# Pooling the PSUM banks, spreading the up projections, and moving an addition to VectorE in a planned attention and MLP kernel

## The chip, the cores and the metric

One core of a Trainium2 chip. The metric is device time in microseconds (us), the median of the runs that are named. The record lists every run of this study as fast; all are compared as fast runs, each with runs of the kernel before on the same chip. TensorE (PE) does the matrix products and leaves them in eight PSUM banks (3 x 2 and 2 x 1 in the kernel before); VectorE (DVE) and ScalarE (ACT) empty the banks (an "evacuation"); GpSimd (POOL) works beside them.

## The reference, cut to what matters

```python
def reference(A_x, ...):                       # x is 1 x 2048 x 512
    def _A_ref(x, wq, wk, wv, wo, beta):       # 32 heads of 16, N = 4 segments of L = 512
        phi = lambda t: jnp.where(t > 0, t + 1.0, jnp.exp(t))
        ...
        for s in range(N):
            logits = jnp.einsum('bhqd,bhkd->bhqk', qs, ks) * scale + mask
            p = _softmax(logits, axis=-1)
            a_dot = jnp.einsum('bhqk,bhkd->bhqd', p, vs)
            pq = phi(qs)
            num = jnp.einsum('bhld,bhde->bhle', pq, M)
            den = jnp.einsum('bhld,bhd->bhl', pq, z)[..., None] + 1e-06
            o = g * (num / den) + (1.0 - g) * a_dot
            pk = phi(ks)
            M = M + jnp.einsum('bhld,bhle->bhde', pk, vs)
            z = z + jnp.einsum('bhld->bhd', pk)
        ...
        return o @ wo
    def _B_ref(x, w_gate, w_up, w_down):       # width 1792 = 14 pieces of 128
        return (_gelu(x @ w_gate) * (x @ w_up)) @ w_down
    x = A_x
    g = _sigmoid((x * gate_w).sum(-1, keepdims=True))
    return g * a + (1 - g) * b
```

Names in what follows: a logit group is q times k for one slot, a pv group is p times v (`a_dot`), an M group adds to M and z, `num` and `zbd` (z as a block-diagonal tile) belong to num and den, a mask is the causal zeroing of p on GpSimd, and a down group is the product with `w_down`.

Per segment there are 14 "up" pieces, each four matmuls of 128x512 on TensorE. So there are 56 up groups in all. phi is needed 12 times, each on a tile of 128x1024.

## The kernel before

The kernel is a list of tasks. A small planner in Python gives each task an engine and a place in that engine's order, from assumed durations; the order is fixed when the program is built. A task can start in the plan only when a buffer of its "ring" is free. PSUM is split into two rings:

```python
plg = ctx.enter_context(tc.tile_pool(name="plg", bufs=3, space=bass.MemoryType.PSUM))    # 3 x 2 banks
pgen = ctx.enter_context(tc.tile_pool(name="pgen", bufs=2, space=bass.MemoryType.PSUM))  # 2 x 1 bank
RINGS = {"lg": 3, "gen": 2, "qT": 3, "kT": 3, "kO": 3, "pT": 12, "E": 1, ...}
```

A logit slot takes two "lg" buffers (a pair of banks for each of two exponentials); nearly everything else shares the two "gen" banks. Slots are kept at least PACE apart:

```python
PACE = 1900
...
    # logit_slot(s, t)
    g = add("PE", 240, fn, prio=0, deps=deps, mode="row", alloc=["lg", "lg"], frees=frees,
            gap=(LT[gi - 1], PACE) if gi > 0 else None)
```

In the dense stage ahead of the first slot stand the q, k, v and gate products of segment 0 and the gate products of all segments (between the last GELU and the first exponential the trace has an ACT_TABLE_LOAD of 1.28 us on ScalarE, so the kernel keeps the two apart). Fourteen up groups stand there too (13 of them run before the first logit group):

```python
for s in range(NSEG):
    ...
    for hp in range(HS // 2):
        gate_pair(s, hp, 41 + 20 * s + hp)
        ...
        if s >= 2:
            up_group(*ups.pop(0), 41.5 + 20 * s + hp)
```

The other 42 are "fillers" between slots: all 28 of segments 1 and 2 in the first segment's slots, then 7, 7 and 0. The addition of phi is on GpSimd:

```python
def f_a(_):
    d = mk()
    nc.gpsimd.tensor_add(d[:, :, :], box["E"][:, :, :], box["Q"][:, :, :])
...
return add("POOL", 2250, f_a, prio=5, deps=[m, q], alloc=[ring], frees=[("E", e), ("Q1", q)])
```

The softmax here doesn't subtract the row's maximum and nothing guards it: scores larger than these inputs give would overflow.

## Time and profile before

| | kernel before |
|---|---|
| time, median of 15 runs | 290.55 us (289.91 to 291.34) |
| span of the profiled run | 289.2 us |
| TensorE, ScalarE, VectorE, GpSimd busy | 94%, 72%, 62%, 45% |
| first and last logit group start | 78.32 and 263.49 us |
| sum of the 79 slot intervals by TensorE's work | 172.3 us |
| excess of the trace over that sum | 12.9 us |

The last three rows are the ledger that the prediction sets up: each interval between logit groups is priced from what TensorE has to do in it, and what the trace has over that is the excess, which is stall but for some 0.8 us of rounding.

A timeline line reads: start in us, duration, engine, line of the kernel, operation, output<-inputs, shapes, xcount, and in brackets how long the engine sat idle before it and what ended that. A line of the list of waits reads: us in total, times, longest.

### The profile page before, as it was taken

The numbers are of one execution on the slowest core, as the hardware profiler recorded it, in microseconds if no ns is written. First come the engines' busy times: TensorE is split into PE (matmuls) and PEld (weight loads), VectorE is DVE, ScalarE is ACT, GpSimd is POOL, SyncE is SP. The second block draws the span as 40 slices with busy tenths as digits, with TensorE's granted clock in tenths as the row PEclk, the third lists the DMA queues.
The fourth block names the chain that finished last, engine by engine and source line by source line (L and its number), as shares of the span: only waits on it lengthen the run. The fifth ranks groups of instructions, "written<-read, shape, count | busy, mean of one in ns | idle before, by whom it ended". The sixth has DMA issues, their size and how long they took to land.

```text
span 289.2 us, 5673 instructions
## 1 busy us (share of the span) xinstructions
PE 272.4 (94%) x2279; PEld 118.1 (41%) x2320; DVE 178.8 (62%) x320; ACT 208.6 (72%) x227; POOL 130.0 (45%) x220
## 2 busy tenths in 40 slices
PE   7999999999998997999989999998899999999994
PEld 4444444444443443343334444333344344344441
DVE  2331212232197899888997786789986973869400
ACT  3634554424497998699998998999899999896021
POOL 8000000015037786755497657554855855556000
PEclk9999999999999999999999999999999999999999
DMA  7974960000001110100001330000000000000011
GB/s 241 325 125 79 363 211 2 0 0 2 0 2 36 36 24 18 39 0 2 0 2 31 27 51 25 14 8 2 0 20 20 0 20 18 22 22 18 20 36 37
DMA packets 22019, 13.74 MB, mean 48 GB/s; under 512 B 14056, under 2 KB 20968, under 8 KB 21992
## 3 DMA queue, kind: packets, MB, share of 16 engines
q1 hardware_dynamic: 21448, 12.85, 17.2%
q10 hardware_dynamic: 544, 0.52, 0.5%
q8 instruction: 18, 0.29, 0.5%
q14 instruction: 9, 0.07, 0.1%
HBM read 8.13 MB, written 2.10 MB: 35 GB/s over the span
## 4 chain that ended last, share of the span: by engine, by line
PE 67%; DVE 17%; SPq 7%; DMA 2%; POOL 2%; issue 2%; ACT 1%; ACTq 0%
PE dn L828 16%; PE up L324 14%; PE gt L324 12%; SPq L233 7%; PE lg L575 7%; PE pv L626 6%; PE dn L833 5%; PE k L324 2%; DVE T L644 2%; PE q L324 2%; DVE vz L176 2%; DVE G L495 2%; DVE Nm L817 2%; POOL pT L607 1%; DVE Tm L813 1%
## 5 line engine op out<-in xcount | busy, mean ns | idle before, releaser
L598 ACT ACTIVATE pT<-lg 128x1024 bf16<-128x1024 f32 x160 | 154.2, 1027 | 15.2 <-PE lg L575 14.0
L607 POOL TENSOR_SCALAR_AFFINE_SELECT pT<-pT 128x512 bf16<-128x512 bf16 (+1 forms) x160 | 93.2, 593 | 72.2 <-ACT pT L598 71.2
L495 DVE TENSOR_TENSOR G<-up,G 128x512 bf16<-128x512 f32 x56 | 38.0, 683 | 41.1 <-PE up L324 41.1
L324 PE MATMUL up<-xT,wup 128*128 128x512 bf16 x213 | 55.2, 380 | 3.1 <-DVE G L495 1.9
L485 ACT ACTIVATE G<-gt 128x1024 bf16<-128x1024 f32 x28 | 28.7, 1023 | 36.1 <-PE gt L324 36.1
L828 PE MATMUL dn<-wdn,G 128*128 128x512 bf16 x213 | 52.2, 380 | 1.9 <-DVE vz L176 0.7
L324 PE MATMUL gt<-xT,wga 128*128 128x512 bf16 x217 | 50.9, 379 | 0.4
L324 PEld LDWEIGHTS <-wga 128*128 128x128 bf16 x224 | 21.8, 98 | 26.2
L324 PEld LDWEIGHTS <-wup 128*128 128x128 bf16 x224 | 19.9, 97 | 27.9 <-issue 8.2
L828 PEld LDWEIGHTS <-G 128*128 128x128 bf16 x224 | 20.2, 98 | 26.9 <-issue 5.9
L456 POOL COPY G<-tt 32x16 f32<-32x16 f32 x16 | 3.1, 195 | 56.9 <-DVE tt L448 56.3
L644 DVE STREAM_TRANSPOSE T<-pv 128x512 f32<-128x512 f32 x32 | 22.7, 711 | 9.0 <-PE pv L626 8.9
L626 PE MATMUL pv<-pT,vz 128*32 128x256 bf16 (+2 forms) x640 | 23.4, 275 | 0.4
L575 PE MATMUL lg<-qT,kT 16*128 16x256 bf16 (+2 forms) x320 | 18.7, 273 | 0.1
L575 PE MATMUL lg<-qT,kO 32*128 32x128 bf16 (+2 forms) x320 | 18.0, 272 | 0.1
L421 PE MATMUL v<-wv,xT 128*128 128x512 bf16 x61 | 15.5, 379 | 2.7 <-DVE vz L176 1.6
L833 PE MATMUL dn<-wo,xT 128*128 128x512 bf16 x63 | 16.2, 379 | 0.2 <-issue 0.2
L626 PEld LDWEIGHTS <-vz 128*32 128x32 bf16 x640 | 12.6, 96 | 8.8 <-issue 1.3
L869 ACT ACTIVATE osb<-dn,omz 128x512 bf16<-128x512 f32 x6 | 4.1, 686 | 16.6 <-PE dn L833 16.6
L324 PE MATMUL q<-xT,wq 128*128 128x512 bf16 x59 | 15.4, 380 | 0.2
L575 PEld LDWEIGHTS <-kT 16*128 16x128 bf16 x320 | 7.3, 92 | 20.0 <-issue 19.3
L699 POOL TENSOR_TENSOR pq<-E,Q 128x1024 bf16<-128x1024 bf16 x6 | 12.8, 2140 | 4.0 <-DVE E L695 4.0
(88 smaller groups left out, 249.9 us busy)
## 6 DMA issues: line engine op xcount, KB each, us to landing
out_dram<-osb SPq DMA_DIRECT2D x16, 128.0 KB, 1.7
wup<-in_B_w_up_dram SPq DMA_DIRECT2D x1, 1792.0 KB, 8.0
wdn<-in_B_w_down_dram SPq DMA_DIRECT2D x1, 1792.0 KB, 13.4
wga<-in_B_w_gate_dram SPq DMA_DIRECT2D x1, 1280.0 KB, 11.1
wq<-in_A_wq_dram SPq DMA_DIRECT2D x1, 512.0 KB, 6.4
wga<-in_B_w_gate_dram SPq DMA_DIRECT2D x1, 512.0 KB
wv<-in_A_wv_dram SPq DMA_DIRECT2D x1, 512.0 KB, 8.3
wo<-in_A_wo_dram SPq DMA_DIRECT2D x1, 512.0 KB, 9.0
```

The lines of the kernel that those rows point to most:

```text
L233: nc.sync.dma_start_transpose(xT[:, fc, s * L:(s + 1) * L], x2[s * L:(s + 1) * L, fc * P:(fc + 1) * P])
L324: nc.tensor.matmul(t, lhsT=W[:, fc, c0:c0 + P], rhs=xT[:, fc, s * L:(s + 1) * L], start=(fc == 0), stop=(fc == FC - 1))
L421: nc.tensor.matmul(t[:, :], lhsT=xT[:, fc, s * L + kt * P:s * L + (kt + 1) * P], rhs=wv[:, fc, :], start=(fc == 0), stop=(fc == FC - 1))
L485: ge = evac("ACT", g, box, lambda e, t: nc.scalar.activation(dst, t[:, :, :], AF.Gelu_apprx_tanh), cost=960, ring="lg")
L495: UPT[(s, hs)] = evac("DVE", g, box, lambda e, t: nc.vector.tensor_mul(G[:, s, hs, :], t[:, :], G[:, s, hs, :]))
L575: nc.tensor.matmul(A[j // 2][:, j % 2, at * P:(at + nq) * P], lhsT=l, rhs=r, start=True, stop=True, tile_position=(32 * j, 0))
L598: nc.scalar.activation(pT[(s, t, h)][:, :, :], A[h][:, :, :], AF.Exp, scale=0.25)
L607: nc.gpsimd.affine_select(out=v, in_=v, pattern=pat, compare_op=ALU.is_ge, fill=0.0, base=0, channel_multiplier=-1)
L626: nc.tensor.matmul(t[32 * j:32 * j + 32, qb * P:(qb + nq) * P], lhsT=vz[s % 2][:, kt, h * VW:h * VW + 32], rhs=pT[(s, t0 + w, j // 2)][:, ...
L644: nc.vector.transpose(TT[key][:, e, :, :].rearrange("p a b -> p (a b)"), t[:, :])
L828: nc.tensor.matmul(t[:, :], lhsT=G[:, s, hs, qt * P:(qt + 1) * P], rhs=wdn[:, hs, :], start=(hs == 0), stop=stop and (hs == HS - 1))
L833: nc.tensor.matmul(t, lhsT=xT[:, c, s * L + qt * P:s * L + (qt + 1) * P], rhs=wo[:, c, :], start=first and c == 0, stop=(c == NCH - 1))
```

## The change

The intent is to let TensorE stall less in the slots. There are 672 lines of diff; the core of it has four parts.

One: all eight PSUM banks in one tile, any single bank for a dense group and any two adjacent ones for half a logit slot. The planner guards the slot's two pairs:

```diff
+SHAPES = {"gen": [(b,) for b in range(NBANK)],
+          "pair": [(b, b + 1) for b in range(NBANK - 1)]}
...
+    ps = pps.tile([P, NBANK, L], F32, name="ps", tag="ps")
...
+        def take(kind, used, at, hold, mode):
+            best = None
+            guard = kind == "gen" and mode != "row" and nleft and due is not None
+            if guard:
+                g = [1e12 if b in used else guess(b) for b in range(NBANK)]
+                lim = due + SLACK
...
+            for q in SHAPES[kind]:
...
```

Two: all 56 up groups between the slots, and a pace that divides the dense work that is left by the slots that are left:

```diff
+NUPS = (28, 10, 9, 9)
-            if s >= 2:
-                up_group(*ups.pop(0), 41.5 + 20 * s + hp)
...
-        g = add("PE", 240, fn, prio=0, deps=deps, mode="row", alloc=["lg", "lg"], frees=frees,
-                gap=(LT[gi - 1], PACE) if gi > 0 else None)
+        g = add("PE", 235, fn, prio=-10, deps=deps, mode="row", alloc=["pair", "pair"], frees=frees)
...
+                if t.mode == "row":
+                    nleft -= 1
+                    due = t0 + max(MINPACE, dense / nleft + 240 + 2 * SWITCH) if nleft else None
```

Three: the addition of phi on VectorE:

```diff
-            nc.gpsimd.tensor_add(d[:, :, :], box["E"][:, :, :], box["Q"][:, :, :])
+            nc.vector.tensor_add(d[:, :, :], box["E"][:, :, :], box["Q"][:, :, :])
...
-        return add("POOL", 2250, f_a, prio=5, deps=[m, q], alloc=[ring],
+        return add("DVE", 650, f_a, prio=5, deps=[m, q], alloc=[ring],
```

Four: a better planner. It first plans, then emits; its assumed durations are nearer to the trace (an exponential 920 ns, was 960); down projections come in pieces of two matmuls; priorities are slot numbers.

## The prediction

> **What bounds the kernel now.** I read four views of the kernel before: the page's busy line, the windows of its three stages, the timeline of TensorE where it runs cleanly and where it does not, and the waits of TensorE.
>
> ```profile
> PE 272.4 (94%) x2279; PEld 118.1 (41%) x2320; DVE 178.8 (62%) x320; ACT 208.6 (72%) x227; POOL 130.0 (45%) x220
> ```
>
> TensorE is busy 94% of the span and nothing else is near it. The windows (span, then busy microseconds of each engine) show three stages: a dense one up to the first logit group at 78.3 us, the slots (80 logit groups, each with two exponentials on ScalarE) up to 264, and the tail.
>
> ```profile
> 0.00:78.00 78.00, 75.28 (x356) 34.33 (x364) 20.34 (x45) 34.33 (x37) 11.44 (x48) 1.00 0.44 125
> 78.00:264.00 186.00, 176.20 (x1797) 74.47 (x1827) 151.86 (x264) 168.94 (x184) 117.01 (x170) 1.00 0.09 17
> 264.00:290.00 26.00, 20.91 (x128) 9.34 (x129) 6.57 (x13) 5.30 (x7) 1.54 (x3) 0.98 0.09 31
> ```
>
> In the slots TensorE is 95% busy by the modelled ends, ScalarE 91%, VectorE 82%. [...]I price its work by starts. A clean stretch of its timeline:
>
> ```profile
> 120.40 0.40 PE L575 MATMUL lg<-qT,kT 16*128 16x512 bf16 x4
> 120.72 0.73 PE L626 MATMUL pv<-pT,vz 128*32 128x512 bf16 x20
> 121.38 1.04 PE L324 MATMUL up<-xT,wup 128*128 128x512 bf16 x4
> 122.35 0.40 PE L575 MATMUL lg<-qT,kT 16*128 16x256 bf16 x12
> ```
>
> From start to start: a logit group takes 0.33 us, a pv group 0.66, and four dense matmuls before a logit group 0.97, which is 4 x 0.216 (the spacing in long dense runs) and 0.10 for the change of tiling. So one slot costs 0.426 + 0.216 per dense matmul + 0.66 per pv group + 0.059 per M matmul. Here 0.426 + 0.864 + 0.66 = 1.95, against 1.95 in the trace. I did this sum for all 79 intervals between logit groups. Most agree within 0.02 us; together they are 172.2 us by the sum and 185.2 in the trace (first logit start 78.32, last 263.49). **The excess of 12.95 us, less 0.8 of systematic rounding (79 x 0.01), is 12.2 us of stall.** It sits in clumps: 1.3 at the first v groups, 0.7 after the first M group, 2.5 at 113 to 120, 2.3 around 142 to 152, 2.5 from 192 to 205, the rest in bits. The worst clump:
>
> ```profile
> 112.72 0.40 PE L575 MATMUL lg<-qT,kO 32*128 32x512 bf16 x4
> 113.35 1.02 PE L324 MATMUL up<-xT,wup 128*128 128x512 bf16 x4 [0.23 <-DVE G L495]
> 115.39 1.02 PE L324 MATMUL up<-xT,wup 128*128 128x512 bf16 x4 [1.02 <-DVE G L495]
> 116.35 0.40 PE L575 MATMUL lg<-qT,kO 32*128 32x256 bf16 x12
> 117.04 1.02 PE L324 MATMUL up<-xT,wup 128*128 128x512 bf16 x3 [0.29 <-DVE G L495]
> 118.23 1.02 PE L324 MATMUL up<-xT,wup 128*128 128x512 bf16 x4 [0.17 <-DVE G L495]
> ```
>
> Each up group waits until VectorE has emptied one of the two single-bank buffers. VectorE had other work queued ahead of that:
>
> ```profile
> 112.01 0.68 DVE L756 TENSOR_TENSOR Mbd<-Macc,bdeb 128x512 bf16<-128x512 f32 x1
> 112.62 0.68 DVE L495 TENSOR_TENSOR G<-up,G 128x512 bf16<-128x512 f32 x1
> 113.22 1.52 DVE L759 TENSOR_TENSOR zbd<-Macc,bd 128x32 bf16<-128x32 f32 x1
> 114.66 0.68 DVE L495 TENSOR_TENSOR G<-up,G 128x512 bf16<-128x512 f32 x1
> ```
>
> The waits of TensorE in the slots name VectorE for nearly all that shows (the two largest):
>
> ```profile
> PE up L324 <- DVE G L495: 1.9, 5, 1.0
> PE v L421 <- DVE vz L176: 1.6, 2, 1.1
> ```
>
> So the bound is TensorE's own work, 277.0 us of the 289.2 (289.2 - 12.2), plus stalls because two buffers are too few when VectorE is late. Where there is no VectorE clump (177 to 190, 205 to 229) the slots run at 1.96 to 2.16 us without stall, so ScalarE keeps up with that pace: an exponential repeats every 0.92 us.
>
> [...]The trace shows 216 in the sustained stream; I use that. [...]zbd takes 1.52 us beside a GpSimd addition of 2.44 us, and 0.20 us in its two other calls.
>
> **The change part by part.**
> 1. Eight pooled banks in place of three pairs and two singles. The logit groups still take two adjacent pairs, but between their uses any bank serves any group. I resolved each TensorE wait of the built program to the instruction that it waits for: nearly all are true users of the same bank or operand, so one large PSUM tile brings no false waits that I can find. Each extra bank buys 0.86 us of VectorE lateness (four dense matmuls), and the visible waits are at most 1.1 us. This should take most of the 12.2 us.
> 2. The up groups leave the dense stage. Before, 13 of them run before the first logit group, so it should come 13 x 0.864 = 11.2 us earlier, at 67.1. They go between the slots: my sum over the built order gives 190.6 us for the 79 intervals (mean 2.41, was 2.18), and 13.9 us after the last logit group (was 21.0). 67.1 + 190.6 + 13.9 = 271.6; before, 78.3 + 172.2 + 21.0 = 271.5. Nothing is saved by this as such: it spreads the same TensorE work and gives ScalarE and VectorE 18 us more in which to do the slots. After the last matmul 4.7 us remain, as before.
> 3. Twelve additions of phi go from GpSimd to VectorE: 12 x 2.12 us = 25.5 off GpSimd. A VectorE addition of half the size repeats every 0.30 to 0.34 us, so about 0.57 each (an estimate), 7 us in all. With 13 more up products (13 x 0.59 = 8) VectorE has about 15 more in the slots, less some 5 for evacuations that the new order gives to ScalarE[...]: (151.9 + 15 - 8) / 205 = 78% against 82%. It isn't the bound, but in the first segment (28 up products, six phi) I count about 50 us of VectorE for 56 of TensorE, 89%.
> 4. ScalarE gets more evacuations: I count 47, 45, 41 and 39 us in the four segments against 56, 52, 44 and 39 of TensorE (to the last logit group). The last two are 94 to 100% full; a late exponential there stalls a logit group.
> 5. Down projections in pieces of two, and num behind den: no new instruction; order only.
>
> The sum: 277.0 us with no stall. I leave 3.5 us of stall, a bit under a third of what there was: 1.5 in the first segment (VectorE at 89%), 1.5 in the last two (ScalarE), 0.5 elsewhere. Span 280.5. The timed median is 1.5 above the profiled span now (290.66 against 289.2), so **282.0 us**, ratio 0.970.
>
> **The rivals.** *ScalarE takes over as the bound in the last two segments.* For it: the count of 94 to 100%. Against: before, the clean stretches ran at 95% ScalarE without stall. If ScalarE's queue slips, 3 to 5 us come back: 285. *VectorE's clumps stay,* because up products and additions are added to its queue while a bank still waits for it, and the order is fixed at build time from assumed durations: a VectorE op that waits 0.6 us for a GpSimd mask delays all behind it. For it: 89% in the first segment. Against: the mean spacing there is 2.8 us, was 2.2. If half the stalls stay: 284.5. *The wait isn't for banks at all:* the v and up groups stall only because VectorE is late as such, and more banks move the stall to a later pv or xT. Then the gain is from spreading alone, and 286 to 288 result, within 2%. I hold that for unlikely because TensorE has no idle stretch that waits for data of pv or xT in the list of waits. *Nearly all stalls go:* 1 us left, 279.5.
>
> **Range and chances.** No stall at all would be 278.5, which is the floor (277.0 + 1.5); half the stall left, 284.6; two thirds, 286.6. Range 279.0 to 286.8. Faster by over 2% needs under 284.9, that is less than 6.4 us of stall: 0.83. Same 0.16, slower 0.01, since the floor itself isn't touched by any part.
>
> **What would show each step right or wrong.** Right: first logit group near 67 us; 216 ns in the dense runs unchanged; the sum of slot excess near 4 us in place of 12.95; waits of TensorE for VectorE products under 1.5 us in all; phi additions of 0.5 to 0.8 us on VectorE; GpSimd near 105 us busy; zbd always near 0.2 us; last matmul start some 4.4 us before the end. Wrong: logit groups waiting for exponentials for more than 3 us (ScalarE is the bound), pv groups waiting for masks, or clumps of up waits over 1 us as before. A different tiling cost or a first logit group later than 69 us would upset the sum itself.

## The result, and the profile after

The changed kernel takes 280.4 us (median of 8 runs, 279.8 to 281.01) against 290.55 before: ratio 0.9649, interval 0.9637 to 0.9661. Ratios here are the mean time of one kernel's runs over that of the other's in the same rounds, so not quite the ratio of the medians. The prediction was 282.0, range 279.0 to 286.8, and "faster" at 0.83.

The page's busy line, and the windows of the three stages (columns: span, then busy microseconds and count of TensorE, weight loads, VectorE, ScalarE, GpSimd, then clock, DMA share, GB/s):

```profile
PE 268.3 (97%) x2280; PEld 116.7 (42%) x2320; DVE 171.0 (61%) x319; ACT 215.0 (77%) x240; POOL 105.3 (38%) x208
```

```profile
0.00:67.00 67.00, 65.31 (x312) 29.56 (x319) 10.76 (x31) 35.54 (x39) 11.47 (x48) 1.00 0.49 145
67.00:264.00 197.00, 192.62 (x1913) 82.49 (x1947) 157.11 (x282) 176.71 (x198) 93.86 (x160) 1.00 0.07 18
264.00:279.00 15.00, 10.42 (x65) 4.63 (x58) 3.09 (x6) 2.75 (x4) 0.00 (x0) 1.00 0.11 37
```

The dense stage and the tail each lost about 11 us, the slots' stage grew by the same, and in it TensorE went from 95% to 98% busy. VectorE is at 80% there (157.11 / 197), ScalarE at 90%. The place that answers to the worst clump before, in TensorE's timeline: the same kind of mix of up groups and slots, now with no wait mark on any line.

```profile
114.02 1.03 PE L441 MATMUL ps<-xT,wup 128*128 128x512 bf16 x4
114.97 0.29 PE L686 MATMUL ps<-qT,kT 16*128 16x256 bf16 x4
115.09 0.28 PE L686 MATMUL ps<-qT,kO 32*128 32x256 bf16 x4
115.31 1.90 PE L441 MATMUL ps<-xT,wup 128*128 128x512 bf16 x8
117.04 0.64 PE L844 MATMUL ps<-vz,pk 128*128 128x136 bf16 x8
117.61 0.40 PE L686 MATMUL ps<-qT,kO 32*128 32x512 bf16 x4
```

VectorE at the spot that answers to the 1.52 us zbd: 0.20 now, with an up product on each side.

```profile
104.13 0.68 DVE L609 TENSOR_TENSOR G<-ps,G 128x512 bf16<-128x512 f32 x1
104.73 0.20 DVE L869 TENSOR_TENSOR zbd<-Macc,bd 128x32 bf16<-128x32 f32 x1
105.48 0.65 DVE L609 TENSOR_TENSOR G<-ps,G 128x512 bf16<-128x512 f32 x1
```

Its other two calls take 0.17 and 0.41 us. And here is the only wait of TensorE on VectorE that the list of waits still has (its other entries are below 0.5 us or are instruction issue). It is the wait for the first memset at the start of the program, which the kernel before has too:

```profile
PE ps L486 <- DVE wdn L364: 1.3, 1, 1.3
```

**The account of the span.** In the profiled run, logit groups start from 66.31 to 260.01 us. The work of the 79 intervals sums to 190.6, the excess is 3.07, the tail's work is 13.85 and 4.2 remain after it: 66.3 + 190.6 + 3.1 + 13.9 + 4.2 = 278.1. Before it was 78.3 + 172.3 + 12.9 + 21.0 + 4.7 = 289.2. TensorE's own work only moved between the stages: 13 up groups or 11.2 us out of the first and 7.1 out of the tail, 18.3 into the slots. Of the 11.1 us that were won, 9.8 are stall in the slots, 0.8 the start and 0.5 what follows the tail.

### The profile page after: what moved, and what is told of

It is laid out like the page before. It is cut to its first block, busy times and chain, and to the rows that moved or that the text cites.

```text
span 278.1 us, 5695 instructions
## 1 busy us (share of the span) xinstructions
PE 268.3 (97%) x2280; PEld 116.7 (42%) x2320; DVE 171.0 (61%) x319; ACT 215.0 (77%) x240; POOL 105.3 (38%) x208
## 5 line engine op out<-in xcount | busy, mean ns | idle before, releaser
L708 ACT ACTIVATE pT<-ps 128x1024 bf16<-128x1024 f32 x160 | 154.2, 1031 | 14.7 <-PE ps L686 12.5
L937 PE MATMUL ps<-wdn,G 128*128 128x512 bf16 x208 | 54.9, 380 | 2.6 <-issue 1.9
L441 PE MATMUL ps<-xT,wup 128*128 128x512 bf16 x218 | 53.0, 380 | 0.4 <-issue 0.2
L609 DVE TENSOR_TENSOR G<-ps,G 128x512 bf16<-128x512 f32 x56 | 37.6, 679 | 18.8 <-PE ps L441 18.5
L441 PE MATMUL ps<-xT,wga 128*128 128x512 bf16 x219 | 48.4, 379 | 0.4 <-issue 0.2
L599 ACT ACTIVATE G<-ps 128x1024 bf16<-128x1024 f32 x28 | 28.7, 1024 | 23.5 <-PE ps L441 22.8
L754 DVE STREAM_TRANSPOSE T<-ps 128x512 f32<-128x512 f32 x32 | 22.8, 712 | 19.1 <-PE ps L736 18.1
L736 PE MATMUL ps<-pT,vz 128*32 128x256 bf16 (+2 forms) x640 | 23.4, 275 | 0.0
L686 PE MATMUL ps<-qT,kT 16*128 16x256 bf16 (+2 forms) x320 | 17.3, 274 | 0.1
L686 PE MATMUL ps<-qT,kO 32*128 32x128 bf16 (+2 forms) x320 | 17.2, 272 | 0.0
L441 PE MATMUL ps<-xT,wk 128*128 128x512 bf16 x43 | 11.9, 380 | 0.3
```

The source lines that it names most:

```text
L441: nc.tensor.matmul(t, lhsT=W[:, fc, c0:c0 + P], rhs=xT[:, fc, s * L:(s + 1) * L], start=(fc == 0), stop=(fc == FC - 1))
L599: ge = evac("ACT", g, box, lambda e, t: nc.scalar.activation(dst, t[:, :, :], AF.Gelu_apprx_tanh), cost=960, ring="pair")
L609: UPT[(s, hs)] = evac("DVE", g, box, lambda e, t: nc.vector.tensor_mul(G[:, s, hs, :], t[:, :], G[:, s, hs, :]))
L686: nc.tensor.matmul(A[j // 2][:, j % 2, at * P:(at + nq) * P], lhsT=l, rhs=r, start=True, stop=True, tile_position=(32 * j, 0))
L708: nc.scalar.activation(pT[(s, t, h)][:, :, :], A[h][:, :, :], AF.Exp, scale=0.25)
L736: nc.tensor.matmul(t[32 * j:32 * j + 32, qb * P:(qb + nq) * P], lhsT=vz[s % 2][:, kt, h * VW:h * VW + 32], rhs=pT[(s, t0 + w, j // 2)][:, ...
```

## The experiments

All were correct on the reference. For each I give the ledger as above, and a cost: the difference of its ratio from the changed kernel's 0.9649, times 290.5 us. Twelve kernels were run, on three chips; the kernel before took 290.49, 291.61 and 290.72 us on them. The intervals leave 0.6 to 0.8 us either way on most costs (1.1 for e8, 1.4 for e5 and e6). Except in e9 and e10 the planner makes a new order for each kernel, so some of each cost can be the luck of one plan; no run measures how much.

| run | time, us | ratio (interval) | first logit | slots' work | excess | tail's work | rest | span |
|---|---|---|---|---|---|---|---|---|
| before | 290.55 | 1 | 78.3 | 172.3 | 12.9 | 21.0 | 4.7 | 289.2 |
| changed | 280.40 | 0.9649 (0.9637, 0.9661) | 66.3 | 190.6 | 3.1 | 13.9 | 4.2 | 278.1 |
| e1 banks split | 285.55 | 0.9825 (0.9806, 0.9844) | 66.4 | 186.3 | 6.6 | 18.2 | 6.0 | 283.5 |
| e2 14 ups dense | 285.75 | 0.9841 (0.9816, 0.9867) | 78.3 | 178.5 | 9.1 | 13.9 | 4.2 | 284.0 |
| e3 adds on GpSimd | 283.96 | 0.9770 (0.9753, 0.9788) | 66.9 | 189.3 | 6.4 | 15.1 | 4.6 | 282.4 |
| e4 all three undone | 293.20 | 1.0090 (1.0072, 1.0107) | 78.7 | 175.5 | 15.7 | 16.9 | 4.6 | 291.3 |
| e5 old, all ups in slots | 296.08 | 1.0141 (1.0097, 1.0186) | 67.5 | 169.7 | 15.1 | 34.8 | 6.4 | 293.5 |
| e6 as e5, pace 2250 | 304.00 | 1.0411 (1.0368, 1.0455) | 67.4 | 188.3 | 24.6 | 16.2 | 5.8 | 302.3 |
| e7 old, adds on VectorE | 290.05 | 0.9940 (0.9918, 0.9963) | 78.4 | 171.6 | 11.8 | 21.6 | 4.6 | 288.1 |
| e8 pairs at fixed places | 285.25 | 0.9770 (0.9733, 0.9807) | 68.0 | 191.3 | 6.9 | 13.2 | 4.7 | 284.1 |
| e9 useless adds | 290.51 | 0.9978 (0.9956, 1.0001) | 66.1 | 190.6 | 11.9 | 13.9 | 4.2 | 286.7 |
| e10 useless memsets | 283.14 | 0.9735 (0.9715, 0.9755) | 66.3 | 190.6 | 6.0 | 13.9 | 4.2 | 281.0 |
| e11 7 ups dense | 281.88 | 0.9693 (0.9672, 0.9715) | 73.6 | 183.3 | 4.3 | 15.1 | 4.2 | 280.5 |
| e12 other plan | 280.29 | 0.9634 (0.9611, 0.9657) | 67.3 | 190.6 | 2.6 | 13.9 | 4.2 | 278.6 |

The theory: the gain is the stall that better buffers remove; spreading the ups by itself saves nothing; the place of the additions counts for little. The rivals: the gain comes from spreading, or from having no GpSimd additions beside VectorE's work.

### One part undone at a time

**e1_split_banks** keeps everything but the pool: three pairs and two singles as before, replanned by the new planner.

```diff
-SHAPES = {"gen": [(b,) for b in range(NBANK)],
-          "pair": [(b, b + 1) for b in range(NBANK - 1)]}
+SHAPES = {"gen": [(6,), (7,)], "pair": [(0, 1), (2, 3), (4, 5)],
+          "any": [(b,) for b in range(NBANK)]}
```

(The "any" shape serves the last output groups, once no logits are left, as before. The opening transposes were put on matching banks.)

> The changed kernel with part 1 alone undone: three fixed pairs for the logit groups and two single banks for everything else, as before; up groups still in the slots, additions still on VectorE, new planner (it plans anew for these banks). My theory (the stalls are too few free banks when VectorE is late): most of the stall comes back, an excess of 7 to 12 us over the sum of TensorE's work in place of 3.1, time 285 to 289. Rival (the spreading of the up groups or the new planner's pacing made the gain): excess stays under 5 us, time 280 to 283.

It costs 5.1 us. The time is at the low end of the first range, the excess of 6.6 us just under it. In the ledger, 3.5 us more is slot stall and 1.8 more follows the tail's work. Waits of TensorE's up groups for VectorE are back, as in the kernel before but smaller:

```profile
PE ps L441 <- DVE G L609: 1.2, 4, 0.6
```

So the pool matters, but it accounts for roughly half the gain, not for "most of the 12.2".

**e2_ups_dense** puts 14 up groups back in the dense stage (pieces of the same lines as in the kernel before):

```diff
-NUPS = (28, 10, 9, 9)
+NUPS = (21, 7, 7, 7)
...
+            if s >= 2:
+                up_group(*ups.pop(0), -958.5 + 20 * s + hp)
```

> The changed kernel with part 2 alone undone: 14 up groups back in the dense stage, so the mean interval of the slots falls from 2.41 to 2.28 us. My theory (spreading saves nothing by itself): 280.5 to 283, excess under 5 us. Rival (spreading is the gain): excess 8 us or more, 286 to 290.

It costs 5.6 us, with eight pooled banks and the additions on VectorE. "Nothing is saved by this as such" falls. The ledger says where: the first logit group is 12.0 us later and the slots have 12.1 less work, an even trade; but the excess is 6.0 us higher. The largest piece of it is in the last segment, whose slots now hold 36.9 us of TensorE work (39.1 in the changed kernel). TensorE and ScalarE there:

```profile
232.53 7.44 ACT L711 ACTIVATE pT<-ps 128x1024 bf16<-128x1024 f32 x8 [0.22 <-PE ps L689]
234.59 0.39 PE L689 MATMUL ps<-qT,kT 16*128 16x512 bf16 x2
235.44 0.53 PE L689 MATMUL ps<-qT,kT 16*128 16x512 bf16 x4 [0.46 <-ACT pT L711]
236.35 0.40 PE L689 MATMUL ps<-qT,kT 16*128 16x256 bf16 x10 [0.39 <-ACT pT L711]
237.27 1.26 PE L739 MATMUL ps<-pT,vz 128*32 128x512 bf16 x20 [0.52 <-ACT pT L711]
238.46 2.24 PE L940 MATMUL ps<-wdn,G 128*128 128x512 bf16 x6
240.63 0.29 PE L689 MATMUL ps<-qT,kT 16*128 16x256 bf16 x4
```

ScalarE runs eight exponentials without a break, 0.93 us each, so a slot takes 1.86 us of ScalarE. Here two logit groups stand next to each other with no dense work between, and the second waits for exponentials. With fewer matmuls to put between slots, ScalarE's time shows. The list of waits has 2.1 us of TensorE waiting for exponentials in all, which the changed kernel doesn't have (0.6), and 1.1 for VectorE.

In this trace TensorE's granted clock is also 0.50 from 236.65 to 240.05 us (1.00 in the 6.8 us before), in this very place: the pv group and the six dense matmuls after it take 3.36 us from start to start (237.27 to 240.63), where the prices give 2.06. So some 1.3 us of this trace's excess is the clock and not a wait (an estimate from these numbers), and without it the last segment has 1.3 us more than in the changed kernel, the other three 1.6, 1.1 and 0.8. The cost of e2 as a whole doesn't hang on the spell: one of the four runs had a mean clock of 1.000 and took 285.75, like the two runs at 0.994 (285.76, 285.63). That spreading matters is shown by the cost; that ScalarE's time is the reason is shown for those 2.1 us of waits, and the rest isn't traced to a cause.

**e3_pool_adds** puts the additions back on GpSimd, with the cost that the kernel before assumed:

```diff
-            nc.vector.tensor_add(d[:, :, :], box["E"][:, :, :], box["Q"][:, :, :])
+            nc.gpsimd.tensor_add(d[:, :, :], box["E"][:, :, :], box["Q"][:, :, :])
...
-        return add("DVE", 650, f_a, prio=5, deps=[m, q], alloc=[ring],
+        return add("POOL", 2250, f_a, prio=5, deps=[m, q], alloc=[ring],
```

> The changed kernel with part 3 alone undone: the twelve phi additions back on GpSimd at 2.12 us each. My theory (VectorE has room[...]): within 1 us of the changed kernel, 279.5 to 281.5. Rival (a GpSimd addition blocks VectorE for up to 2 us and that is what stalled TensorE): 283 to 286, with single VectorE instructions of 1.1 to 1.5 us beside the additions.

It costs 3.5 us; I had expected it within 1. In the timeline a VectorE product with two SBUF operands starts 0.11 us after a GpSimd addition and ends 0.55 us after that has ended, and TensorE's next group waits behind it:

```profile
99.79 2.12 POOL L809 TENSOR_TENSOR pkT<-E,Q 128x1024 bf16<-128x1024 bf16 x1
99.90 2.56 DVE L772 TENSOR_TENSOR N<-T,r 128x512 bf16<-128x512 f32 x1
103.12 0.63 PE L844 MATMUL ps<-vz,pk 128*128 128x136 bf16 x8 [1.47 <-DVE vz L288]
```

The same product has a median of 0.69 us in the changed kernel. The sum is plain: VectorE is busy 171.3 us here and 171.0 in the changed kernel, although it has lost the 12 additions (8.9 us) and got only three other evacuations more (about 2.1). So some 7 us of VectorE's time is lost (an estimate from these four numbers). By kind, in summed durations: the instructions with two SBUF inputs take 3.3 us more than in the changed kernel without its additions, and those of the kind TENSOR_SCALAR, which read one tile and a number or a column, 2.7 more (two additional evacuations left out). Handing the additions to GpSimd relieves VectorE of nothing.

**e4_all_undone** undoes the three at once, and keeps only the new planner.

> All three parts undone together, so that only the new planner is left (pacing by the work that remains, new assumed durations, down projections in twos). My theory: near the kernel before, 287 to 291, excess 9 to 13 us. Rival (the planner is the gain): 281 to 284.

It is slower than the kernel before by 0.9%, and above what my theory had expected. So the new planner gives nothing by itself; whether the three parts need it to give what they give was not run. The three single costs are 5.1 + 5.6 + 3.5 = 14.2 us, all three together 12.8: nearly additive. There is no one part that holds the gain.

### One part done alone on the kernel before

**e5_old_ups** moves the ups into the slots of the kernel before; **e6_old_ups_paced** does the same with a slower fixed pace:

```diff
-            if s >= 2:
-                up_group(*ups.pop(0), 41.5 + 20 * s + hp)
...
+        short = [[(0, hs) for hs in range(HS)] + [(1, hs) for hs in range(HS)],
+                 [(2, hs) for hs in range(10)],
+                 [(2, hs) for hs in range(10, HS)] + [(3, hs) for hs in range(5)],
+                 [(3, hs) for hs in range(5, HS)]][s]
```
```diff
-PACE = 1900
+PACE = 2250
```

> The kernel before with the up groups moved out of the dense stage (all 56 between the slots), old planner with its fixed least interval of 1.9 us, old banks, GpSimd additions. The old planner fills the slots as tightly as before (my sum: 169.7 us for the 79 intervals) and leaves the rest, 34.8 us, after the last slot. If the gain is from having the up groups between the slots as such: 285 to 287. If only an even spread gives it: 288 to 292, the excess in the slots as large as before, about 13 us.

> As the last, but with the least interval raised from 1.9 to 2.25 us, so that the slots are spread (187.8 us for 79 intervals, 16.2 after). If slots with room for ScalarE and VectorE need no pooled banks and no new planner: excess 5 to 8 us, 283 to 286. If two single banks stall TensorE wherever VectorE is late: excess over 10 us, 287 to 290.

Both are slower than before, by 1.4% and 4.1%, and above what either theory had expected. In e5 the slots' work is 169.7 us and the tail's is 34.8: with a fixed pace the slots run ahead and the dense work piles up behind the last one, where no exponential lies beside it. A slower pace mends that (188.3 and 16.2), but then the slots stall for 24.6 us, with single waits of TensorE of 1.8 us for a GpSimd mask and 2.2 for a v evacuation. Why it stalls that much I did not settle. Its four runs also all had a lower mean clock (0.980 to 0.989); the trace has two spells at half clock in the slots (0.50 from 95.15 to 98.50 us and from 136.15 to 139.50), which can make up 3.4 of the 24.6 us at most.

**e7_old_vector_adds** moves only the additions in the kernel before (the e3 diff the other way round).

> The kernel before with the twelve phi additions on VectorE alone. After the third experiment (where VectorE instructions of 2.6 us stood beside GpSimd additions) I expect a gain here too: 1.5 to 4 us, 286.5 to 289. If the additions only cost VectorE time in the tight slots of the old plan: 290 to 292.

It gains 1.7 us (0.6%), at the low end of what I had expected, with an excess of 11.8 in place of 12.9. That the relief of VectorE is worth less here because two banks are the limit anyway is a guess; no run separates it from the old planner.

### What about the pool counts

**e8_half_pool** lets singles go anywhere, but pairs only to four fixed places.

```diff
-          "pair": [(b, b + 1) for b in range(NBANK - 1)]}
+          "pair": [(b, b + 1) for b in range(0, NBANK, 2)]}
```

> The changed kernel with logit pairs only on even banks (0-1, 2-3, 4-5, 6-7) and single groups still on any bank. If sharing the banks is what counts: within 1 us of the changed kernel, 279.5 to 281.5. If the free placing of pairs counts: 282 to 285.

It costs 3.5 us, though the interval is wide (2.4 to 4.6) and 1.7 us of the profiled span is a wait for the beta transfer ahead of the first logit group. The excess is 6.9. The time is just above the second range. So the sharing of all eight banks is not enough; where a pair may lie counts as well.

### Why the place of the additions matters

e3 leaves two explanations. VectorE's instructions with two SBUF inputs last longer beside a GpSimd instruction that reads SBUF (A), or GpSimd is simply busy and its masks come late (B). Under A, GpSimd work that reads should cost more than as much work that only writes; under B the two should cost the same. That makes a test. Both of these kernels are the changed kernel with useless GpSimd work before each addition of phi; one reads, the other only writes.

```diff
+            for i in range(2):                                                  # e9_idle_adds
+                nc.gpsimd.tensor_add(dmy[:, :], wq[:, i, :], wq[:, 2 + i, :])
```
```diff
+            for i in range(5):                                                  # e10_idle_memsets
+                nc.gpsimd.memset(dmy[:, :], 1.0)
```

> The changed kernel, order on TensorE, VectorE and ScalarE untouched, plus twelve useless GpSimd additions (two of 128x512 from SBUF, some 2.1 us in all) at the places where the phi additions used to be; nothing uses their result. Theory A (a GpSimd addition that reads SBUF blocks VectorE instructions with two SBUF inputs): VectorE instructions of 1.1 us and more come back, 282 to 285. Theory B (it is only that masks queue behind the addition): the same time here as in the next run. Theory C (in the third experiment it was the phi addition's own latency): no change, 280 to 281.

> As the last with five GpSimd memsets of 128x512 (about 2.1 us, they read nothing) in place of each pair of useless additions. Theory A: VectorE not blocked, only masks delayed, 280.4 to 281.5, clearly less than the last. Theory B: the same as the last. Theory C: no change in either.

The two are the same load to the digit: 24 adds of 1347 ns and 60 memsets of 539 ns, 32.3 us of GpSimd each. TensorE's order is the same in all three kernels. The adds cost 9.6 us, the memsets 2.5, both above what I had expected for A. The same spot in the timelines, VectorE and GpSimd, first with the adds (e9):

```profile
149.05 2.44 POOL L812 TENSOR_TENSOR dmy<-wq 128x512 bf16<-128x512 bf16 x2
149.11 1.38 DVE L778 TENSOR_TENSOR N<-N,Nm 128x512 bf16<-128x512 bf16 x1
150.41 1.64 DVE L810 TENSOR_TENSOR pq<-E,Q 128x1024 bf16<-128x1024 bf16 x1
153.32 0.73 PE L737 MATMUL ps<-pT,vz 128*32 128x512 bf16 x20 [2.04 <-DVE Tm L927]
```

then with the memsets (e10):

```profile
146.74 2.85 POOL L812 MEMSET dmy<- 128x512 bf16 x5
146.82 0.41 DVE L778 TENSOR_TENSOR N<-N,Nm 128x512 bf16<-128x512 bf16 x1
147.15 0.68 DVE L810 TENSOR_TENSOR pq<-E,Q 128x1024 bf16<-128x1024 bf16 x1
149.11 0.73 PE L737 MATMUL ps<-pT,vz 128*32 128x512 bf16 x20 [0.17 <-DVE Tm L927]
```

Beside the adds, two VectorE instructions take 3.02 us together; beside the memsets, 1.09. The pv group behind them waits 2.04 us in the one and 0.17 in the other. Over the whole run VectorE is busy 183.5 us with the adds and 174.9 with the memsets, against 171.0 without either, with the same instructions in the same order. By kind, in summed durations, the 77 instructions with two SBUF inputs take 45.4 us without either, 54.0 with the adds and 46.3 with the memsets; the 59 of the kind TENSOR_SCALAR (one tile with a number or a column, nearly all in SBUF) 24.4, 29.5 and 27.9. So A is shown for most of it: 7.1 of the 9.6 us is what reading costs over writing, and most of what lengthens beside reading alone is in the two-input instructions (54.0 less 46.3, 7.7 us of the 8.6 between 183.5 and 174.9). The other 2.5 is what the memsets cost, and it is not all B. Instructions with one SBUF input got longer beside the memsets too (the maximum Q of phi_k has a mean of 0.56 us against 0.40). Which share of the 2.5 is that, and which is late masks, stays open.

One thing mixes into e9. Five of its twelve runs have a mean clock of 0.999 or 1.000 and take 289.0 us on average; the seven at 0.991 to 0.994 take 291.0. So a lower clock goes with 2.0 us in those runs. By the five others alone the cost is 8.4 us, and reading costs 5.9 over writing. The profiled run is one of the five.

### How far to spread

**e11_ups_half** leaves seven ups in the dense stage (`NUPS = (28, 7, 7, 7)`, and `if s >= 3:` in the loop of e2). **e12_plan** tries another division and holds pv groups back longer, to stand next to logit groups.

```diff
-NUPS = (28, 10, 9, 9)
+NUPS = (26, 10, 10, 10)
...
-                    if t.mode == "col" and mode == "full" and nleft and t0 - since < 2200:
+                    if t.mode == "col" and mode == "full" and nleft and t0 - since < 3500:
```

> The changed kernel with 7 of the 56 up groups in the dense stage (0 in the changed kernel, 14 in the second experiment, which took 285.75 us with one spell of halved clock worth 1.7 us). If the loss grows with what the slots lack in room for ScalarE: about 282. If it comes from single unlucky places in the plan: anywhere from 280.5 to 286, without order.

> The changed kernel with 26, 10, 10 and 10 up groups in the four segments (was 28, 10, 9, 9) and a pv group held back up to 3.5 us (was 2.2) for a place right behind a logit group, to save the 0.12 us that each of nine lone pv groups costs. Expected gain 0.5 to 1.5 us: 279 to 280 on a chip where the changed kernel takes 280.4. If the plan is at its noise, 280 to 281.5.

None in the dense stage is 280.4 us, seven is 281.88, fourteen is 285.75: the more the slots have to share out, the better, and the second seven cost more than the first. That is what I had expected if the loss grows with the room that the slots lack. (1.2 us of e11's profiled span is a later start, 0.9 of that a wait for the beta transfer.) e12 has 0.5 us less excess in its one profile but a first logit group 1.0 later; its interval overlaps the changed kernel's. I don't count it as an improvement. No version beat the changed kernel.

## Why the prediction was right or wrong

**The bound held.** TensorE's own work plus stall is the time, before and after. The dense runs stay at 0.216 us, the sum of slots and tail by these prices is 204.5 us and the trace is within 3.1 of it in the slots, and the first logit group came at 66.3 (67.1 predicted). TensorE no longer waits a microsecond anywhere for a bank or a product, zbd takes 0.17 to 0.41 us, GpSimd is busy 105.3 us and the additions take 0.73 to 0.74 on VectorE.

**The size of the stall was close, in part by luck.** Predicted 3.5 us left, measured 2.3 (3.07 less 0.8 of rounding). It isn't where I put it. The first segment was to stall 1.5 us for VectorE at 89%: it is at 85% (47.99 busy of 56.26) and its excess is 0.26, all rounding. The last two were to stall 1.5 for ScalarE: their excess is 1.8, or 1.4 without rounding. But four intervals of the third segment and two of the second have 0.11 to 0.12 each where a pv group stands between two dense pieces: as I read it one more change of tiling than my sum counted (0.10 in the clean stretches), not a stall. The other terms: the start is 0.8 us shorter and what follows the tail 0.5, neither foreseen, so the span is 2.4 below the predicted 280.5. Against that, a timed run is 1.7 us above its own span, not 1.5, and the profiled run was, with one other, the fastest of eight, 0.6 below their median. Together 280.4 in place of 282.0.

**"Nothing is saved by this as such" failed** (part 2). It is true of TensorE's sum, which is all that I priced. But the stall depends on how the work is spread: with 14 ups in the dense stage the excess is 9.1 us (some 1.3 of it the clock), with seven 4.3, with none 3.1. The sentence that followed it, that spreading gives ScalarE and VectorE 18 us more for the slots, was the mechanism, and I gave it no number.

**"This should take most of the 12.2 us" was too much for the pool** (part 1). Undone alone it costs 5.1 us, of which 3.5 are slot stall.

**What VectorE loses beside GpSimd was mis-sized** (part 3). My sum has 8 us off, 5 of it for evacuations; the other 3 were my estimate of what VectorE's instructions would get shorter with no GpSimd additions beside them. I took the additions to be a shift of 7 us of work onto an engine with room (8.9 by their durations), and so in e3 expected less than 1 us. They cost 3.5 us when put back: VectorE then loses some 7 us beside them, late in its queue and in clumps, where TensorE waits. The one zbd line that I showed was the sign, and I did not add up the others.

**The rivals.** ScalarE as the bound did not come about in the changed kernel, but in e2, where slots hold less dense work, it shows in the last segment (1.4 of the 2.1 us of waits for exponentials). "The wait isn't for banks at all" was wrong as I put it, since splitting the banks costs 5 us; its second half, that some of the gain is spreading, was right. The prediction was therefore right in its time by a sum whose total was sound, while three parts share what it gave mostly to one.

**What stays open:** why the kernel before gets slower when only the ups move (e6 has 24.6 us of excess), what makes up most of e2's excess, whether the parts need the new planner, and how the loss to memsets in e10 divides.

## What to carry to other kernels

When TensorE is busy to 95%, price its work by starts and call the rest stall; then ask of each part of a change what it does to the stall, even where it moves no work. Slack between slots, places to put results, and a VectorE with no GpSimd additions beside it each cost 3.5 to 5.6 us here when taken away, and the slack was of use only with the rest: the ups alone made the kernel before slower, with its old planner. Before handing work to GpSimd to relieve VectorE, add up how long VectorE's instructions last beside it, those with two SBUF inputs first: here 8.9 us of additions handed over bought no VectorE time at all (busy 171.3 us in e3 against 171.0).

## What the runs show of the hardware

- VectorE beside GpSimd: in e3 one 128x512 product took 2.56 us beside a GpSimd addition of 2.12, against a median of 0.69 in the changed kernel. 32.3 us of GpSimd additions add 12.5 us of VectorE busy time (e9, 183.5 against 171.0), 32.3 of memsets 3.9 (e10, 174.9). The instructions with two SBUF inputs grew by 8.6 us in the one and 0.9 in the other.
- Dense matmuls of 128x512, with a weight load per matmul, start every 216 ns, in both kernels.
- Spells of half clock: the granted clock was 0.50 in e2 from 236.65 to 240.05 us, in e4 from 135.95 to 139.25, and in e6 from 95.15 to 98.50 and from 136.15 to 139.50. In the 3.35 to 3.40 us before each it was 1.00, and TensorE was busy 2.56 us of 3.40 in e2, much of it in small tiles, 1.26 of 3.35 in e4, and 1.52 of 3.35 and 1.18 of 3.40 in e6. TensorE's longest wait there in e2 was 0.46 us. What sets a spell off, the runs don't say. What a spell costs varies: the runs of e9 with a lower mean clock are 2.0 us longer, while the two of e2 at 0.994 are no longer than the one at 1.000, though the spell stretches some 1.3 us of work in its trace.
- Where groups of different tilings meet, TensorE took some 0.10 us more in the clean stretches (0.97 us for four dense matmuls ahead of a logit group, 4 x 0.216 without), and 0.11 to 0.12 where a pv group stood alone. That the change of tiling is the reason is an inference from these sums.
- An addition of two bf16 tiles of 128x1024 took 2.14 to 2.19 us on GpSimd (means, kernel before) against 0.73 to 0.74 on VectorE (means, changed kernel), 2.9 to 3.0 times.
